# Two of nine blocks take the first MLP layer as seven block products, with state banks returned and remnant units joined

## The chip, the cores and the metric

The kernel runs on one core of a Trainium2 chip. A core has five engines that run side by side, each with its own queue of instructions in a fixed order: TensorE (PE in the profile, its weight loads PEld) multiplies matrices into PSUM, VectorE (DVE) and ScalarE (ACT) compute elementwise, GpSimd (POOL) computes elementwise in SBUF and issues some DMAs, SyncE (SP) issues the others. PSUM has eight banks of 128 x 512 float32. The metric is the device time of one execution in microseconds (us), as the median of several.

## The reference

The inputs are q, k, v of 8 batches, 8 heads, 576 positions and 64 features, and two weight matrices. The first part is a retention: scores with a decay per head, masked to the past, times v. The second is an MLP with the gate h * cos(h) on 4608 tokens.

```python
scores = scale * np.matmul(q, k.transpose(0, 1, 3, 2))
Dmat = np.where(rel >= 0, gamma[:, None, None] ** rel[None, :, :], 0.0)
ret = np.matmul(scores * Dmat[None], v)          # x: [4608, 512]
h = x @ w_in                                     # w_in: [512, 2048]
g = h * np.cos(h)
out = g @ w_out                                  # w_out: [2048, 512]
```

## The kernel before

**Blocks and units.** The tokens are split into nine blocks of 512. Blocks 0 to 7 consist of two units each: a unit is 256 positions of one batch, handled in 64-position chunks with a running state (k transposed times v), so that scores are only needed near the diagonal. Block 8 collects the last 64 positions of all batches; its two remnant units are (0,2) and (1,2). For each unit `load` (line 463) brings q, k and v as float32 into staging tiles `stgq`, `stgk`, `stgv`; POOL casts k and weights q and v by the decay into bf16 tiles (`unit`, lines 454 and 496); k and q are transposed on TensorE for the first blocks and by DMA later. `scores` and `outputs` build "sessions" of small matmuls (line 563), in four quadrants of the array at once: scores into two banks, a mask by VectorE into `pt` tiles (line 599), outputs into two banks, ScalarE's copies into the block's input tile `xt`. The states accumulate in two PSUM banks `ST` that are reserved for the whole kernel; ScalarE copies them to SBUF (`snap`).

**The MLP.** `mlp1` computes the first layer of a block for one of 16 slices of 128 hidden features: four matmuls of 512 columns into a bank (256 columns in blocks 0 to 2, two halves apart), ScalarE's sine with a shift of pi/2 into `cb` (line 745), and VectorE's product of bank and `cb` into the gated tile `gt` (line 748). The second layer of block 0 is plain (`plain2`, line 776). Blocks 1 to 8 take the second layer by seven block products instead of eight (`wino2`, line 862, after Strassen and Winograd): sums of blocks of the gated tile (lines 823 and 829, tiles `s`, on VectorE), sums of blocks of w_out made once (`wsums`, tiles `tw`), seven products P1, P2, P6, P5, P7, P3, P4 into three banks A, B and C, of which ScalarE snapshots three into `sn`, and VectorE adds bank and snapshot into the output tile `os` (line 874). `store` (line 761) sends it out by SP.

**The order.** All of this is a graph of tasks. `Graph.run` is a list planner: it gives each task an estimated start from a modelled duration, free engines, free buffers and a due time (`prio`), and the kernel issues every engine's instructions in the order of these starts. `graph` sets the due times: in round j the second layer of block j is due beside the first layer of block j + 1 and the attention of block j + 2, over a period of 28.8 us. `POOLS` holds the number of buffers of each kind. The planner models the fetching of TensorE's instructions (`FETCH`, `left`), and `warm` fills planned gaps early in the kernel with matmuls on a tile of ones (line 401). The weights w_in and w_out come in four parts each through POOL's DMA queue (`load_w`, lines 717 and 721), each behind a gate: a load that must have landed first.

## Time and profile before

| | |
|---|---|
| median of 3 runs | 301.96 us (301.09 to 302.47) |
| the profiled execution | 301.62 us, its span 299.9 us |
| matmuls of the first layer, 512 columns | 384, 95.4 us busy |
| the same, 256 columns | 384, 49.0 us busy |
| gate products on VectorE, 512 columns | 96, 688 ns each |
| sines on ScalarE, 512 columns | 96, 689 ns each |
| output DMAs | 16 of 512 KB, 4 of 128 KB, 2 of 256 KB |
| granted TensorE clock | 1.000 |

A busy matmul is longer than its slot, since matmuls overlap: the distance between starts is what counts. In the rows of groups, "out<-in" names the tiles written and read, "xN" the number of instructions, and "mean ns" the time that one is shown with. A chain row gives start, length, engine, tile and line.

### The profile page before, as it was taken

The page shows a single profiled execution, that of the slowest core. Times are in us where ns is not written, and L with a number is a line of the kernel's source. Part 1 is how long each engine was busy: PE and PEld are TensorE (multiplying, and loading weights), DVE is VectorE, ACT ScalarE, POOL GpSimd, SP SyncE. Part 2 cuts the span into 40 slices and gives each one's busy share as a digit, 9 for nine tenths or more (in the row PEclk, how much of TensorE's full clock was granted, in tenths as well). Part 3 has the DMA queues.
Part 4 walks back from the last instruction along what each step waited for, and adds up shares of the span by engine and source line. Part 5 has one row for each costly group of instructions (what it writes and reads, how often), then busy time and mean ns, then how long its engine had stood idle before and what let it go on. Part 6 is the DMA issues. An engine that isn't in the chain of part 4 may idle for free.

```text
span 299.9 us, 9086 instructions
## 1 busy us (share of the span) xinstructions
PE 285.2 (95%) x3809; PEld 202.7 (68%) x3815; DVE 213.0 (71%) x379; ACT 169.7 (57%) x315; POOL 101.4 (34%) x125
## 2 busy tenths in 40 slices
PE   6789888999999999999999999999999999999994
PEld 6667665666788876766676667666766666666683
DVE  2776495659985889697868686959777666667721
ACT  5369876556667565645655565466565555545420
POOL 3821960665825614825363515172100000000000
PEclk9999999999999999999999999999999999999999
DMA  7999789999999799997999986892103000300115
GB/s 199 252 203 274 202 129 236 280 200 299 207 251 297 151 194 281 214 227 210 229 280 232 244 188 94 194 236 53 24 2 140 2 2 2 140 2 0 70 73 140
DMA packets 101640, 49.87 MB, mean 166 GB/s; under 512 B 43488, under 2 KB 97248, under 8 KB 101600
## 3 DMA queue, kind: packets, MB, share of 16 engines
q1 hardware_dynamic: 97376, 45.10, 63.6%
q0 software_dynamic: 4224, 4.19, 8.8%
q8 instruction: 30, 0.49, 0.7%
q14 instruction: 10, 0.08, 0.1%
HBM read 36.70 MB, written 9.44 MB: 154 GB/s over the span
## 4 chain that ended last, share of the span: by engine, by line
PE 78%; DMA 14%; POOL 5%; issue 1%; SPq 0%; ACT 0%; DVE 0%; DVEq 0%
PE bk L737 35%; PE bk L862 33%; DMA stgq<-in_q_dram 8%; PE bk L563 6%; DMA wout<-in_moe_w_out_dram 3%; DMA win<-in_moe_w_in_dram 3%; PE bk L776 2%; POOL qnat L496 2%; POOL natv L496 2%; PE st L563 1%; POOL natk L454 1%; SPq L463 0%; POOL win L717 0%; POOL wout L721 0%; DVE qnat L496 0%
## 5 line engine op out<-in xcount | busy, mean ns | idle before, releaser
L745 ACT ACTIVATE cb<-bk,cpi 128x256 bf16<-128x256 f32 (+1 forms) x192 | 108.3, 583 | 82.0 <-PE bk L737 79.9
L737 PE MATMUL bk<-xt,win 128*128 128x256 bf16 (+1 forms) x768 | 144.2, 326 | 1.0 <-DMA win<-in_moe_w_in_dram 0.7
L748 DVE TENSOR_TENSOR gt<-bk,cb 128x256 bf16<-128x256 f32 (+1 forms) x192 | 103.8, 555 | 54.9 <-ACT cb L745 47.8
L737 PEld LDWEIGHTS bk<-xt,win 128*128 128x128 bf16 x768 | 72.3, 98 | 39.7 <-DVE pt L599 1.4
L496 POOL TENSOR_TENSOR natv<-stgv,wv 128x512 bf16<-128x512 f32 x36 | 37.7, 1070 | 37.0 <-PE bk L563 20.6
L599 DVE TENSOR_TENSOR pt<-bk,tr 128x512 bf16<-128x512 f32 x68 | 42.7, 682 | 5.5 <-PE bk L563 5.4
L496 POOL TENSOR_TENSOR qnat<-stgq,wq 128x512 bf16<-128x512 f32 x32 | 35.0, 1112 | 15.9 <-DMA stgq<-in_q_dram 15.3
L454 POOL CAST natk<-stgk 128x512 bf16<-128x512 f32 x34 | 21.3, 653 | 55.8 <-DMA stgk<-in_k_dram 44.8
L862 PE MATMUL bk<-wout,gt 128*128 128x256 bf16 x256 | 32.7, 273 | 0.0
L862 PE MATMUL bk<-tw,s 128*128 128x256 bf16 x256 | 32.7, 273 | 0.0
L862 PE MATMUL bk<-wout,s 128*128 128x256 bf16 x256 | 32.4, 273 | 0.0
L862 PEld LDWEIGHTS bk<-tw,s 128*128 128x128 bf16 x256 | 24.9, 98 | 8.1
L862 PEld LDWEIGHTS bk<-wout,gt 128*128 128x128 bf16 x256 | 24.7, 98 | 6.4
L862 PEld LDWEIGHTS bk<-wout,s 128*128 128x128 bf16 x256 | 24.7, 98 | 6.1
L453 ACT ACTIVATE xt<-bk 128x512 bf16<-128x512 f32 x36 | 23.5, 728 | 0.5 <-PE bk L563 0.5
L874 DVE TENSOR_TENSOR os<-bk,sn 128x512 f32<-128x512 f32 x24 | 16.4, 683 | 10.4 <-PE bk L862 10.4
L453 ACT ACTIVATE sn<-bk 128x512 f32<-128x512 f32 x24 | 14.3, 597 | 13.8 <-PE bk L862 13.8
L862 PE MATMUL bk<-tw,gt 128*128 128x256 bf16 x128 | 16.4, 273 | 0.0
L776 PE MATMUL bk<-wout,gt 128*128 128x512 bf16 x58 | 15.3, 380 | 0.6 <-issue 0.3
L862 PEld LDWEIGHTS bk<-tw,gt 128*128 128x128 bf16 x128 | 12.5, 98 | 4.0
L829 DVE TENSOR_TENSOR s<-gt 128x1024 bf16<-128x1024 bf16 x16 | 12.8, 800 | 0.2
L563 PE MATMUL bk<-qt,kt 64*64 64x128 bf16 (+1 forms) x576 | 12.1, 217 | 0.4 <-ACT xt L453 0.4
(58 smaller groups left out, 187.7 us busy)
## 6 DMA issues: line engine op xcount, KB each, us to landing
stgk<-in_k_dram SPq DMA_DIRECT2D x16, 512.0 KB, 7.0
stgq<-in_q_dram SPq DMA_DIRECT2D x16, 512.0 KB, 6.9
stgv<-in_v_dram SPq DMA_DIRECT2D x16, 512.0 KB, 6.9
out_dram<-os SPq DMA_DIRECT2D x16, 512.0 KB, 3.3
win<-in_moe_w_in_dram POOLq DMA_DIRECT2D x4, 512.0 KB, 9.0
wout<-in_moe_w_out_dram POOLq DMA_DIRECT2D x4, 512.0 KB, 10.0
stgk<-in_k_dram SPq DMA_DIRECT2D x8, 128.0 KB, 3.4
stgq<-in_q_dram SPq DMA_DIRECT2D x8, 128.0 KB, 3.5
```

The costliest lines, as they stand in the source:

```text
L453: return self.one(eng, dur, lambda e: e.activation(dst(), src(), AF.Copy), r=r, w=w, **kw)
L454: return self.one(eng, dur, lambda e: e.tensor_copy(dst(), src()), r=r, w=w, port=True, **kw)
L496: self.one(eng, 610 if eng == "dve" else 1000, lambda e, out=out, inp=inp, tab=tab, col=col, hs=hs: e.tensor_tensor(out(), inp(), ap(tab, ...
L563: return lambda e: e.matmul(out(), lhs(), rhs(), start=start, stop=True, skip_group_check=True)
L599: self.one("dve", 610, lambda e, r=r, b=b, pt=pt: e.tensor_tensor(ap(self.at(pt), 1024, 0, 128, 512 * r, [64 * ny * ny, 8 // ny // ny], [1 ...
L737: inst = e.matmul(ap(self.at(bk), 512, 0, 128, 0, [1, n]), ap(self.WIN, 4 * DFF, 0, 128, c * DFF + 128 * f, [1, 128]), ap(self.at(xt), 204 ...
L745: self.one("act", 70 + n, lambda e: e.activation(ap(self.at(cb), TB, 0, 128, 0, [1, n]), ap(self.at(bk), 512, 0, 128, 0, [1, n]), AF.Sin, ...
L748: self.one("dve", 75 + n / 0.96, lambda e: e.tensor_tensor(ap(self.at(gt), NF * TB, 0, 128, f * TB + 256 * h0, [1, n]), ap(self.at(bk), 51 ...
L776: inst = e.matmul(self.at(bk).ap(), ap(self.at(gt), NF * TB, 0, 128, f * TB + 256 * half + 128 * tt, [1, 128]), ap(self.WOUT, NF * DM, 0, ...
L829: self.one("dve", 610, lambda e, i=i, q=q, x=x, y=y, op=op: e.tensor_tensor(sv(i, q), x(), y(), op), r=r, w=[(S_[i, q],)], port=True, name ...
L862: inst = e.matmul(ap(self.at(bank), 512, 0, 128, 256 * tt, [1, 256]), l(f, tt), rr(f), start=(first and f == 0 and tt == 0), stop=True, sk ...
L874: self.one("dve", 610, lambda e: e.tensor_tensor(view(h, c), ap(self.at(bank), 512, 0, 128, 0, [256, 2], [1, 256]), ap(self.at(sn[name]), ...
```

## The change

**Seven products in the first layer.** From `SEVEN = 7` on, a block's first layer is computed by `seven1` in four groups; a group covers two slices of each half of the hidden features. x and w_in are seen as 2 x 2 blocks (halves of the tokens or of the hidden features, halves of the model features). `wsums1` makes the sums of w_in once (three into new tiles `tx`, one in place over the second half of the hidden features), `xsums` those of the block's input (three into `xs`, one in place in `xt`), all on VectorE. Each of the seven products is four matmuls of 256 columns. ScalarE snapshots three banks; VectorE adds bank and snapshot into a new float32 tile `h` in SBUF; ScalarE takes the sine of it, and VectorE the product. The fourth quarter is gated out of its bank, as before. All products of the gate are on VectorE, as before.

**The second layer.** The third sum of the gated tile is now written in place over the tile; for block 7 the sums go to POOL. In the last block bank A is two banks, and its last product, copies and stores go by halves of tokens.

**Sessions and banks.** The remnant units share one session for their scores and one for their outputs. The state banks are buffers of the pool of eight, free again after their last use.

**Planner and pools.** Instruction fetch is modelled otherwise, warming matmuls have 512 columns instead of 128, w_out is gated by q of unit (1,1) instead of v, and unit (2,0) by the third part of w_out instead of the second. A write of an `h` tile waits for VectorE's own earlier readers of it.

```diff
-            deps += [d for d in readers if d.eng != eng or d.sem or sem]
+            deps += [d for d in readers if d.eng != eng or d.sem or sem or k[0] == "h"]
...
-    AHEAD, FETCH = 2000, 3000
+    AHEAD, FETCH = 2000, 6500
...
+    @staticmethod
+    def fill(gap, seen):
+        return int(0.6 * (gap - 150) / 220 if seen else (gap - 300) / 430)
...
-                if e == "pe" and t.count > left[0]:
-                    s = max(s, left[1] - t.dur * left[0] / t.count)
+                if e == "pe" and t.count:
+                    k = (seen + t.count - 443) // 256
+                    if k >= 0 and 443 + 256 * k > seen and k in asked:
+                        s = max(s, asked[k] + self.FETCH - t.dur * (443 + 256 * k - seen) / t.count)
...
-                dma_free = max(dma_free, s + (1700 if e == "pool" else 1150)) + t.dma
+                dma_free = max(dma_free, s + (2400 if e == "pool" and s > dma_free - 700 else 1700 if e == "pool" else 1150)) + t.dma
...
-    POOLS = dict(bk=6, stgk=3, stgv=3, stgq=3, natk=3, natv=3, qnat=2, kt=3, qt=3, pt=4, sba=3, sbb=3, sbr=8, xt=2,
-                 gt=2, s=9, cb=3, os=3, sn=3)
+    POOLS = dict(bk=8, stgk=2, stgv=2, stgq=2, natk=3, natv=3, qnat=2, kt=3, qt=3, pt=2, sba=3, sbb=3, sbr=8, xt=2,
+                 gt=2, s=6, cb=4, os=2, sn=5, xs=3, h=4)
...
-        self.ST = [nc.alloc_psum_tensor(f"st{i}", [128, 512], F32) for i in range(2)]
...
-                    self.warm(int((gap - 300) / 110 if not warm else 0.6 * (gap - 150) / 57))
+                    self.warm(max(1, self.G.fill(gap, warm)))
...
-                inst = e.matmul(ap(self.at(self.wb), 512, 0, 128, 0, [1, 128]), self.ONE.ap(), self.ONE.ap(),
+                inst = e.matmul(self.at(self.wb).ap(), self.ONE.ap(), ap(self.ONE, 128, 0, 128, 0, [0, 4], [1, 128]),
...
+        if join is not None:
+            join.append((u, phases))
+            if len(join) < 2:
+                return
+            self.emit_lanes("ses/%d.%d" % u, prio, [x for _, y in join for x in y], alloc=[self.tiles[v]["pt", 0] for v, _ in join])
...
+            self.emit_lanes("ses:%d.%d" % u, prio, [(x[0], x[2], x[3], []) for x in join]
+                            + [(x[1], x[2], x[3], [i]) for i, x in enumerate(join)], alloc=[xt])
...
+    def wsums1(self):
...
+        for c in range(2):
+            for dst, x, y, r, w in (
+                    (lambda c=c: t(1, c), lambda c=c: b(0, 1, c), lambda c=c: b(0, 0, c), slabs(0) + slabs(1), [("x1", c)]),
+                    (lambda c=c: t(2, c), lambda c=c: b(1, 1, c), lambda c=c: t(1, c), slabs(1) + [("x1", c)], [("x2", c)]),
+                    (lambda c=c: t(4, c), lambda c=c: b(1, 0, c), lambda c=c: t(2, c), slabs(0) + [("x2", c)], [("x4", c)]),
+                    (lambda c=c: b(0, 1, c), lambda c=c: b(1, 1, c), lambda c=c: b(0, 1, c), [], slabs(1))):
+                self.one("dve", 610, lambda e, dst=dst, x=x, y=y: e.tensor_tensor(dst(), x(), y(), ALU.subtract),
+                         r=r, w=w, port=True)
+
+    def xsums(self, j):
...
+                (1, lambda: a(0, 1), lambda: a(1, 1), self.xkeys(j, (1,)), ALU.add),
+                (2, lambda: sv(1), lambda: a(0, 0), self.xkeys(j, (0,)) + [(X[1],)], ALU.subtract),
+                (4, lambda: a(1, 0), lambda: sv(2), self.xkeys(j, (0,)) + [(X[2],)], ALU.subtract)):
...
+    def seven1(self, j, g, prio, span):
...
+        A, Bb, C = Buf("bk"), Buf("bk"), Buf("bk")
+        sn = {n: Buf("sn") for n in ("p1", "u2", "p5")}
...
+        def gate(h, n, bank, name):
...
+            if name:
+                src = Buf("h")
+                key = (src,)
+                self.one("dve", 610, lambda e: e.tensor_tensor(
+                    self.at(src).ap(), self.at(bank).ap(), self.at(sn[name]).ap(), ALU.add),
+                    r=[(bank,)] + [(sn[name], x) for x in range(2)], w=[key])
+            self.one("act", 620 if name else 580, lambda e: e.activation(
+                self.at(cb).ap(), self.at(src).ap(), AF.Sin, bias=self.CPI.ap(), scale=1.0), r=[key, ("cpi",)], w=[(cb,)])
+            self.one("dve", 610, lambda e: e.tensor_tensor(dst(), two(src), two(cb), ALU.mult),
+                     r=[key, (cb,)], w=[(gt, 8 * n + 2 * g + f, h) for f in range(2)])
+
+        for n, p in enumerate((1, 2, 6, 5, 7, 3, 4)):
...
+            self.one("pe", 4 * 109, mm, r=keys, w=[(bank,)], alloc=[gt], prio=prio + span * n / 7, name=f"M{p}_{j}", count=8.4)
+            if p == 1:
+                snap("p1", A)
+            elif p == 2:
+                gate(0, 0, Bb, "p1")
+            elif p == 6:
+                snap("u2", A)
+            elif p == 5:
+                snap("p5", C)
+            elif p == 7:
+                gate(1, 1, A, "p5")
+            elif p == 3:
+                gate(0, 1, C, "u2")
+            else:
+                gate(1, 0, A, None)
...
     def wino2(self, j, base, span):
...
+        eng, dur = ("pool", 2000) if self.SEVEN <= j < NTB - 1 else ("dve", 610)
+        S_ = {(i, q): Buf("s") for i in (1, 2, 4) for q in range(2)}
...
+            self.one(eng, dur, lambda e, q=q: e.tensor_tensor(a(0, 1, q), a(0, 0, q), a(0, 1, q), ALU.subtract),
+                     r=ak(0, 0, q), w=ak(0, 1, q), port=True, name=f"S3_{j}")
...
+        last = j == NTB - 1
+        A, Bb, C = [Buf("bk") for _ in range(1 + last)], [Buf("bk")], [Buf("bk")]
...
+            halves = last and p == 4
...
-                if j == NTB - 1:
+                if last:
                     self.store(j, 1, os[1], (256, 512))
-                    self.store(j, 1, os[1], (0, 256))
+                    for i in range(2):
+                        self.store(j, 1, os[1], (0, 256), (i,))
...
+        self.stb = [Buf("bk"), Buf("bk")]
...
+            if us[0][1] == 2:
+                self.unit(us[1])
+                one, two = [], []
+                for u in us:
+                    self.scores(u, prio, [], 0, one)
+                for u in us:
+                    self.outputs(u, prio + 10000, [], two)
+                return
...
-        gate = [(st["v", (1, 1)], 0)]
+        gate = [(st["q", (1, 1)], 0)]
...
-        self.unit((2, 0), gate=[("wout", 1, 0)])
+        self.unit((2, 0), gate=[("wout", 2, 0)])
...
+            if j + 1 == self.SEVEN:
+                self.wsums1()
+            if j + 1 >= self.SEVEN and not last:
+                self.xsums(j + 1)
+                for g in range(4):
+                    self.seven1(j + 1, g, base + PER * g / 4, PER / 4)
+            elif not last:
```

## The prediction

> **What bounds the kernel now.** I read the page first (busy shares and slices), then the busy time by stage, then the chain that ended last, then VectorE's own rows. The first fence is from the page, the second the stages: each row has start:end, length, and busy time with count of PE, PEld, DVE, ACT, POOL, then clock, DMA share and GB/s.
>
> ```profile
> span 299.9 us, 9086 instructions
> PE 285.2 (95%) x3809; PEld 202.7 (68%) x3815; DVE 213.0 (71%) x379; ACT 169.7 (57%) x315; POOL 101.4 (34%) x125
> ```
>
> ```profile
> 0.00:17.20 17.20, 12.39 (x264) 10.78 (x264) 8.03 (x28) 8.81 (x15) 10.63 (x25) 1.00 1.00 222
> 17.20:61.00 43.80, 38.49 (x577) 28.18 (x577) 29.83 (x66) 31.37 (x71) 19.24 (x24) 1.00 1.03 218
> 61.00:229.10 168.10, 167.84 (x2325) 117.52 (x2327) 132.73 (x223) 98.47 (x182) 71.48 (x77) 1.00 0.87 195
> 229.10:258.20 29.10, 28.93 (x371) 18.97 (x370) 20.39 (x32) 15.33 (x24) 0.00 (x0) 1.00 0.10 38
> 258.20:282.60 24.40, 24.40 (x164) 15.74 (x162) 17.18 (x26) 12.10 (x18) 0.00 (x0) 1.00 0.08 28
> 282.60:295.70 13.10, 13.10 (x121) 11.52 (x118) 4.84 (x7) 3.08 (x5) 0.00 (x0) 1.00 0.28 90
> 295.70:299.90 4.20, 0.03 (x1) 0.00 (x0) 0.00 (x0) 0.60 (x1) 0.00 (x0) 1.00 0.71 187
> ```
>
> The reader is to see three things. From 61 us to 295.7 TensorE (PE) waits 0.43 us in all, so there the time is the sum of its matmuls. Before 61 us it idles 4.8 and 5.3 us. After its last matmul 4.2 us of copying and storing follow. Block 7's first layer runs in the row 229.1 to 258.2, beside block 6's second layer and the two remnant units; block 8's in 258.2 to 282.6, beside block 7's second layer. VectorE (DVE) is busy 70% of both; POOL does nothing.
>
> The chain of waits is TensorE from 60.85 us to its last matmul (start, length, count):
>
> ```profile
> 61.82 1.31 PE bk L737 x12
> ...
> 262.67 0.86 PE bk L737 x4
> 263.53 0.87 PE bk L862 x8
> ...
> 282.62 13.11 PE bk L862 x120
> ```
>
> Four 512-column matmuls of the first layer take 0.86 us (0.216 each), twelve of 256 columns 1.31, and 120 of 256 columns in the second layer, each with its own weights, 13.11: 0.109 each. Half the columns cost half, so products of blocks lose nothing by their size.
>
> **VectorE's prices.** Timeline of VectorE, then durations by tile (minimum/median/maximum, ns):
>
> ```profile
> 214.15 0.69 DVE L823 TENSOR_TENSOR s<-gt 128x1024 bf16<-128x1024 bf16 x1
> 214.88 0.69 DVE L823 TENSOR_TENSOR s<-s,gt 128x1024 bf16<-128x1024 bf16 x1
> 216.69 2.48 DVE L599 TENSOR_TENSOR pt<-bk,tr 128x512 bf16<-128x512 f32 x4
> ```
>
> ```profile
> L823 DVE TENSOR_TENSOR s<-s,gt x16: 681/691/1421, 73.7 to 284.9; 128x1024 bf16<-128x1024 bf16 x16
> L829 DVE TENSOR_TENSOR s<-gt,s x16: 679/684/1294, 83.1 to 285.6; 128x1024 bf16<-128x1024 bf16 x16
> L874 DVE TENSOR_TENSOR os<-bk,sn x24: 674/681/693, 86.3 to 294.0; 128x512 f32<-128x512 f32 x24
> L496 POOL TENSOR_TENSOR natv<-stgv,wv x36: 1032/1042/1492, 8.8 to 209.3; 128x512 bf16<-128x512 f32 x36
> ```
>
> An instruction is shown with 0.69 us, but four in a queue end after 2.48, so the pitch is 0.60; one that reads its predecessor starts 0.73 after it. Sums with both inputs in SBUF run to 1.42 us and POOL's products to 1.49, where the two engines meet; L874, with one input in a PSUM bank, never exceeds 0.693.
>
> **The change, part by part.** The sum stands against the profiled execution: 301.62 us, 299.9 of it span and 1.7 around it. The median of the three runs is 301.96, 0.34 above, which I add at the end. Times at which a transfer landed are from the trace's records of the DMAs.
>
> *First layer of blocks 7 and 8.* Removed per block: 16 x 4 matmuls x 0.216 = 13.8 us. Added: 4 groups x 7 products x 4 matmuls x 0.109 = 12.2. All of it lies on the path: 2 x 1.6 = 3.2 us less.
>
> *Remnant units joined.* In the timeline their four sessions push the next matmul back by 0.38 and 0.92 us (231.8, 236.6) and again 0.38 and 0.91 (246.3, 251.2): 2.6 us. Joined, the half sessions hide each other's 0.3 us between the main and the cross part, and two seams of 0.11 (a slot of 0.97 instead of 0.86) go. Ends 0 and -0.8; I take -0.5. Four banks are now wanted at once for them; eight are there, with the two state banks back.
>
> *ScalarE.* 24 more snapshots at 0.597 (row sn<-bk, 597 ns) make 14.3 us beside 27.4 busy of 53.5: room, costed at nothing. If that cover went, each would hold the next product of its bank.
>
> *VectorE.* Added in the two stages: 24 additions of a bank and its snapshot at 0.60 = 14.4; eight block sums of the input at 0.42 (nearest row: the copy of 128x512 bf16, 420 ns; between 0.3 and 0.69) = 3.4; two sums of w_in in place, 1.4. Removed: block 7's eight sums, which go to POOL, 8 x 0.69 = 5.5. So 20.4 + 17.2 = 37.6 us becomes 51.3, or some 48.5 when everything queues at the pitch, beside a TensorE need of 53.3 - 3.7 = 49.6. VectorE is then as full as TensorE. Queued behind each addition are the sine of ScalarE (which reads h), the snapshots in ScalarE's order behind that sine, and TensorE's next product into the same bank. The new order of VectorE on itself for h waits for an instruction already ahead of it in the queue and costs nothing.
>
> *POOL beside it.* Eight sums of 1024 columns have no row; by the 1.04 us of 512 columns they take 2.05 each, 16.4 in all, between 0.69 (VectorE's own) and 2.4. Three of four gate products now have both inputs in SBUF (h and cb), as the rows that went to 1.42 had. One that finds POOL at work waits for the rest of its 2.05, 1.0 on average. Ends for TensorE: 0, as with the blocked sums of before (1.29 at 130.3, 1.35 at 208.6), which left no gap on it, and 5.3 (worked out as a rival below). I take +1.2, near the end of those rows, because the second layer's products, 0.87 each, stand between those of the first.
>
> The Trainium skill (SBUF — State Buffer, section "Who interferes with whom") has a rule that speaks against the change: a VectorE instruction with two SBUF inputs and a GpSimd instruction that reads SBUF exclude each other for a whole instruction, and one with a single SBUF input is free of it. The trace agrees: 1.42 and 1.49 us where both are at work, 0.693 at most for L874. By that rule alone 24 products would be exposed and the sum would be the slower rival's; by the uncovered rows it would be 1.2 us lower than mine.
>
> *Sums of w_in.* Six more go wherever VectorE is free once w_in has landed, from 26.6 us on: 6 x 0.69 = 4.1 in a stage where VectorE is busy 29.8 of 43.8. Ends 0 and +1; +0.2.
>
> *The start.* w_out is asked for when q of unit (1,1) has landed (34.85) instead of v (36.38): its four requests (3.0 us on POOL) can go ahead of POOL's two q products (2.06, from 35.16). Either w_out lands up to 2.0 us sooner, or that unit's scores come 3.0 later; SP's loads of unit (2,0) now wait for the third w_out part instead of the second (47.05, 2.5 us before the third), which cancels the gain. The planner's other view of instruction fetch and longer, fewer warming matmuls (103 of 128 columns now) reorder everything before 61 us. What it could win is bounded by the idle 5.3 us there, of which "issue" has 1.8. Ends -2.5 and +1.5; I take -0.6, a third of the issue time.
>
> *Smaller pools.* Output tiles three to two: the store of 135.77 has landed at 139.67, the next sum into that tile is at 147.3; at the end 284.08 against 287.03. Costed at nothing for these leads. Staging three to two, score tiles four to two: units are some 14 us apart; nothing, at most +2 should a load come late, since 0.26 us idle in 61 to 229 shows no other reserve.
>
> *The tail.* The last product is finished by halves of tokens, copied and stored so. The copy shrinks from 0.60 to about 0.38 (128x256 row, sba<-st, 383). But SP issues six requests from 292.99 to 297.69, some 0.64 each when they queue, and there will be eight. Request seven and eight then start about E+1.5 to E+2.2 after TensorE's end E and land 2.3 later, as against E+3.87 now. Ends -0.5 and +0.6; I take +0.2.
>
> Sum: 301.62 - 3.2 - 0.5 + 1.2 + 0.2 - 0.6 + 0.2 = 298.9, plus 0.3 to the median: **299.2 us**.
>
> **The rivals.** *VectorE and POOL hold each other (slower).* While POOL's eight sums run, each lets one gate product through: 2.05 + 0.60 us for a product and an addition that otherwise take 1.20, so 8 x 1.45 = 11.6 us on VectorE, 48.5 + 11.6 = 60.1 against 49.6. TensorE can fill 5.2 us of that with block 8's products that need no late sum (six slots of 0.87), so about 5.3 is lost: 301.6 - 3.7 + 0.2 + 0.2 + 5.3 = 303.6, 303.9 with the median (the start costed at nothing). For it: VectorE's 48.5 of 49.6 us, and an order on TensorE that is fixed beforehand, so that one late product holds all behind it. Against: POOL's first four sums can start when half of block 7 is gated, some 13 us before its second layer begins, and so meet fewer products. It is slower than the median by 0.5% from a stall of 4.9 us on. Chance 0.22.
>
> *The stall eats the gain (within 0.5%).* A smaller stall, 1.9 to 4.9 us: 300.5 to 303.5, say 301.8. Bank A of each group is written, read, written four times; a turn takes 0.2 + 0.6 + 0.2 us, of which a product of 0.44 covers half, and the second layer's 0.87 must cover the rest. Chance 0.18.
>
> *The start gains too (faster still).* If 2.0 to 2.5 us of the idle before 61 us go and no engine stalls: 301.6 - 3.2 - 0.8 - 2.2 + 0.3 = 295.7. For it: 10 us idle before 61. Against: loads and POOL set the chain there. Chance 0.15.
>
> *TensorE doesn't get shorter.* If the seven products ran at more than 0.123 each (13.8/112), nothing would be saved. The 1.31 us row excludes that but for a few in a hundred, held in the second rival.
>
> **How the numbers follow.** The forecast has 0.45, with its own range 297.5 to 300.4. About 0.5% (1.5 us) is what a measurement of this kernel tells from no change: 300.45 and 303.47. Faster: 0.45 + 0.15 = 0.60; same 0.18; slower 0.22. The range that leaves out one in ten on each side is 295.5 to 304.0.
>
> **What would show it.** Right: about 224 matmuls of 256 columns on the new line at 0.109 pitch, TensorE idle under 2 us between 229 us and its end, which comes at 292 to 293; POOL at 16 us there. Wrong: products on VectorE above 1 us whose start falls into a POOL sum, PE waiting for DVE or ACT in stretches of 0.5 us and more; a start in which TensorE idles more than 10 us up to 61 us; loads that release TensorE after 61 us; last store over 4 us after the last matmul.

## The result and the profile after

The changed kernel takes **310.99 us** (median of 6, 308.44 to 311.8) against 301.84 for the kernel before (median of 6, 301.09 to 304.0): ratio 1.0285, 95% interval 1.0247 to 1.0322. It is slower; the forecast was 299.2 us with a range up to 304.0. The profiled execution of the changed kernel took 308.44 us, the least of its six, with a span of 306.6 us against 299.9.

The first lines of the profile's page of the changed kernel:

```profile
span 306.6 us, 9125 instructions
PE 284.8 (93%) x3834; PEld 207.3 (68%) x3834; DVE 236.3 (77%) x412; ACT 179.7 (59%) x342; POOL 123.2 (40%) x133
```

TensorE is as busy as before (285.2 us then), VectorE by 23 us and POOL by 22 us more. The stages of the changed kernel, with the columns of the earlier table (start:end, length, busy time with count of PE, PEld, DVE, ACT, POOL, then clock, DMA share, GB/s):

```profile
0.00:17.20 17.20, 13.08 (x193) 6.94 (x194) 8.80 (x29) 8.82 (x15) 10.65 (x25) 1.00 1.00 224
17.20:61.00 43.80, 39.22 (x570) 27.42 (x568) 31.31 (x67) 30.68 (x70) 21.41 (x25) 1.00 1.08 221
61.00:232.20 171.20, 168.55 (x2331) 117.87 (x2330) 134.17 (x228) 98.62 (x183) 72.08 (x76) 1.00 0.86 190
232.20:290.20 58.00, 52.59 (x644) 45.19 (x643) 55.52 (x80) 37.88 (x67) 19.03 (x8) 1.00 0.10 38
290.20:301.60 11.40, 11.39 (x104) 9.83 (x102) 6.53 (x11) 3.29 (x8) 0.00 (x0) 1.00 0.22 69
301.60:306.60 5.00, 0.00 (x0) 0.00 (x0) 0.00 (x0) 0.38 (x1) 0.00 (x0) 1.00 0.62 158
```

The third row ends where block 7's first layer begins: at 232.2 us, 3.1 us later than before, with 2.65 us of idle TensorE where there was 0.26. The fourth row is the new first layer: TensorE is idle for 5.41 of its 58.0 us, VectorE's instructions cover all but 2.5 us (time spent waiting for POOL included, see below), and POOL works 19 us. The last row, after the last matmul, has grown from 4.2 to 5.0 us. What TensorE waited for in blocks 7 and 8 (view of waits of PE from 228 to 292 us; total, times, longest):

```profile
PE bk L881 <- DVE h L867: 2.7, 3, 1.7
PE bk L1015 <- DVE gt L872: 1.7, 1, 1.7
PE bk L881 <- DVE xs L814: 0.8, 1, 0.8
PE bk L881 <- ACT sn L463: 0.2, 1, 0.2
```

L881 are the seven products of the first layer, L1015 those of the second. All but 0.2 us of the 5.4 is waiting for VectorE. Its timeline there (start, length, tile, and at the end the idle time before):

```profile
251.35 1.34 DVE L872 TENSOR_TENSOR gt<-h,cb 128x512 bf16<-128x512 f32 x1 [0.23 <-ACT cb L870]
...
253.80 1.41 DVE L872 TENSOR_TENSOR gt<-h,cb 128x512 bf16<-128x512 f32 x1
...
256.94 3.35 DVE L872 TENSOR_TENSOR gt<-h,cb 128x512 bf16<-128x512 f32 x2
260.20 1.27 DVE L867 TENSOR_TENSOR h<-bk,sn 128x512 f32<-128x512 f32 x2
...
264.81 2.23 DVE L872 TENSOR_TENSOR gt<-h,cb 128x512 bf16<-128x512 f32 x1
266.96 2.33 DVE L814 TENSOR_TENSOR xs<-xt,xs 128x512 bf16<-128x512 bf16 x1
...
272.36 2.01 DVE L872 TENSOR_TENSOR gt<-h,cb 128x512 bf16<-128x512 f32 x1
```

and POOL's, which has eight instructions there, the sums of block 7's gated tile (four of them shown):

```profile
250.00 2.13 POOL L972 TENSOR_TENSOR s<-gt 128x1024 bf16<-128x1024 bf16 x1 [36.44 <-DVE gt L872]
252.21 2.45 POOL L972 TENSOR_TENSOR s<-s,gt 128x1024 bf16<-128x1024 bf16 x1
...
257.17 2.56 POOL L977 TENSOR_TENSOR s<-gt,s 128x1024 bf16<-128x1024 bf16 x1
264.37 2.13 POOL L972 TENSOR_TENSOR s<-gt 128x1024 bf16<-128x1024 bf16 x1 [4.63 <-DVE gt L872]
```

Every long instruction of VectorE starts inside one of POOL's sums and ends some 0.55 us, nearly its own time, after that sum (the `xs` sum 0.27): 251.35 + 1.34 = 252.69 against POOL's 250.00 + 2.13 = 252.13; 264.81 + 2.23 = 267.04 against 266.50; the pair at 256.94 ends at 260.29 against 259.73. Against the lengths where nothing blocks (0.68 for a product, 1.28 for two, 0.41 for the `xs` sum) the lines above lose 0.66 + 0.73 + 2.07 + 1.55 + 1.92 + 1.33 = 8.3 us. The durations by tile tell which instructions suffer (minimum/median/maximum, ns):

```profile
L872 DVE TENSOR_TENSOR gt<-h,cb x24: 674/684/2604, 243.3 to 290.8; 128x512 bf16<-128x512 f32 x24
L872 DVE TENSOR_TENSOR gt<-bk,cb x8: 674/680/692, 241.5 to 291.4; 128x512 bf16<-128x512 f32 x8
```

The same product of the same size runs up to 2604 ns when both inputs lie in SBUF (`h`, `cb`) and never above 692 when one lies in a PSUM bank (`bk`). The Trainium skill (SBUF — State Buffer, section "Who interferes with whom") has it so: a VectorE instruction with two SBUF inputs and a GpSimd instruction that reads SBUF exclude each other for a whole instruction. The trace agrees, with 2604 against 692 ns.

### The profile page after: what moved, and what is told of

Its sections match the earlier page's. It is cut to its first block, busy times and chain, and to the rows that moved or that the text cites. A ratio compares the mean times of both kernels' runs of the same rounds, so it can differ in the third digit from the quotient of the medians.

```text
span 306.6 us, 9125 instructions
## 1 busy us (share of the span) xinstructions
PE 284.8 (93%) x3834; PEld 207.3 (68%) x3834; DVE 236.3 (77%) x412; ACT 179.7 (59%) x342; POOL 123.2 (40%) x133
## 3 DMA queue, kind: packets, MB, share of 16 engines
q0 software_dynamic: 4224, 4.19, 8.5%
## 5 line engine op out<-in xcount | busy, mean ns | idle before, releaser
L772 ACT ACTIVATE cb<-bk,cpi 128x256 bf16<-128x256 f32 (+1 forms) x160 | 86.5, 565 | 65.2 <-PE bk L764 64.6
L764 PE MATMUL bk<-xt,win 128*128 128x256 bf16 (+1 forms) x640 | 113.3, 316 | 3.2 <-DMA win<-in_moe_w_in_dram 0.8
L775 DVE TENSOR_TENSOR gt<-bk,cb 128x256 bf16<-128x256 f32 (+1 forms) x160 | 81.1, 526 | 42.9 <-ACT cb L772 40.1
L1015 PE MATMUL bk<-wout,gt 128*128 128x256 bf16 x384 | 49.4, 273 | 1.7 <-DVE gt L872 1.7
L1015 PEld LDWEIGHTS bk<-wout,gt 128*128 128x128 bf16 x384 | 36.7, 98 | 9.1 <-DVE gt L872 2.0
L463 ACT ACTIVATE sn<-bk 128x512 f32<-128x512 f32 (+1 forms) x50 | 27.5, 580 | 21.2 <-PE bk L1015 12.2
L1015 PE MATMUL bk<-tw,s 128*128 128x256 bf16 x256 | 32.5, 273 | 0.0
L1015 PEld LDWEIGHTS bk<-tw,s 128*128 128x128 bf16 x256 | 25.0, 98 | 6.3
L872 DVE TENSOR_TENSOR gt<-h,cb 128x512 bf16<-128x512 f32 x24 | 22.4, 951 | 1.1 <-ACT cb L870 1.1
L870 ACT ACTIVATE cb<-h,cpi 128x512 bf16<-128x512 f32 x24 | 16.9, 721 | 6.9 <-DVE h L867 6.8
L1035 DVE TENSOR_TENSOR os<-bk,sn 128x512 f32<-128x512 f32 (+1 forms) x25 | 16.4, 659 | 4.2 <-PE bk L1015 4.2
L1015 PE MATMUL bk<-tw,gt 128*128 128x256 bf16 x128 | 16.4, 273 | 0.0
L1015 PE MATMUL bk<-wout,s 128*128 128x256 bf16 x128 | 16.4, 273 | 0.0
L867 DVE TENSOR_TENSOR h<-bk,sn 128x512 f32<-128x512 f32 x24 | 15.8, 678 | 0.5 <-PE bk L881 0.5
```

The source lines that it names most:

```text
L463: return self.one(eng, dur, lambda e: e.activation(dst(), src(), AF.Copy), r=r, w=w, **kw)
L764: inst = e.matmul(ap(self.at(bk), 512, 0, 128, 0, [1, n]), ap(self.WIN, 4 * DFF, 0, 128, c * DFF + 128 * f, [1, 128]), ap(self.at(xt), 204 ...
L772: self.one("act", 70 + n, lambda e: e.activation(ap(self.at(cb), TB, 0, 128, 0, [1, n]), ap(self.at(bk), 512, 0, 128, 0, [1, n]), AF.Sin, ...
L775: self.one("dve", 75 + n / 0.96, lambda e: e.tensor_tensor(ap(self.at(gt), NF * TB, 0, 128, f * TB + 256 * h0, [1, n]), ap(self.at(bk), 51 ...
L867: self.one("dve", 610, lambda e: e.tensor_tensor(self.at(src).ap(), self.at(bank).ap(), self.at(sn[name]).ap(), ALU.add), r=[(bank,)] + [( ...
L870: self.one("act", 620 if name else 580, lambda e: e.activation(self.at(cb).ap(), self.at(src).ap(), AF.Sin, bias=self.CPI.ap(), scale=1.0) ...
```

## The experiments

Theories at the start: (A) POOL's eight sums hold up VectorE's products, and this costs nearly everything; (B) VectorE is simply too full, whoever makes the sums; (C) the start and the planner cost it; (D) the seven products do not save what was worked out. Each time stands against runs of the kernel before on the same chip, and "excess" is the difference to their median. An excess is known to about 1 us, and to 2 at most where only four executions stand behind it (the runs without seven products, with the old gates, with POOL's sums known, and with short sums at 70 us).

**POOL's sums, an eighth as wide.** The order of every queue is that of the changed kernel; only POOL's instructions are shorter (seven eighths of each sum are left out).

```diff
+        sw = 32 if eng == "pool" else 256
...
-            return ap(self.at(gt), NF * TB, 0, 128, (8 * k + 4 * q) * TB + 256 * h, [TB, 4], [1, 256])
+            return ap(self.at(gt), NF * TB, 0, 128, (8 * k + 4 * q) * TB + 256 * h, [TB, 4], [1, sw])
```

> POOL's eight sums for block 7's second layer cover 128 of 1024 columns (the rest of those sums is left out, so the output is not the reference's); every order and every wait stays as in the changed kernel. Theory A (the wait of VectorE's products for POOL's 2.1 to 2.6 us sums is what costs): the products of h and cb fall to 0.68 us each from up to 2.2, TensorE's idle time after 228 us falls from 6.4 us to under 1.5, and the time falls by 4 to 6 us against the changed kernel, to about 305 median. Rival B (VectorE's load alone, 100% busy from 228 us on, is what costs): TensorE still idles 4 us or more there and the time falls by less than 2 us, to 309 or more.

Measured: 303.84 us (ratio 1.0055, interval 1.0024 to 1.0087), 7.2 us below the changed kernel. VectorE's group and the stage, durations and windows:

```profile
L872 DVE TENSOR_TENSOR gt<-h,cb x24: 678/682/694, 242.5 to 283.5; 128x512 bf16<-128x512 f32 x24
```

```profile
232.20:290.20 58.00, 58.00 (x704) 51.57 (x703) 51.76 (x86) 40.56 (x73) 4.08 (x8) 1.00 0.13 47
```

The longest product falls from 2604 to 694 ns and TensorE has no idle time in the stage. With the same order and the same instructions, the length of POOL's sums is the only thing that differs, so (A) is shown for the 5.4 us of idle time in this stage. What the medians show beyond that is not explained by it; the two profiled executions also differ at 74 us, where the changed kernel's has a gap of 1.88 us and this one none (below). VectorE is still busy 51.8 of 58 us, which speaks against (B).

**The sums back on VectorE.**

```diff
-        eng, dur = ("pool", 2000) if self.SEVEN <= j < NTB - 1 else ("dve", 610)
+        eng, dur = "dve", 610
```

> Block 7's eight sums go back to VectorE, POOL does nothing there. Theory A: VectorE gets 8 x 0.6 to 0.69 = 5 us of work and loses 8.4 us of waits; the time falls by 2 to 4 us against the changed kernel, to 307 to 309. Rival B: VectorE, already full, is 5 us longer, and the time rises by 2 to 5 us, to 313 or more.

Measured: 304.50 us (1.0078, 1.0045 to 1.0111), 6.5 below the changed kernel and more than (A) had expected. The stage's window:

```profile
232.20:290.20 58.00, 58.00 (x703) 51.48 (x702) 55.99 (x95) 41.20 (x72) 0.00 (x0) 1.00 0.14 51
```

VectorE is busier than in the changed kernel (55.99 against 55.52 us, of which 8.3 were waiting), yet TensorE does not wait in this window. (B) falls: load alone was absorbed. The same can be seen over equal work, from the first matmul of block 7's first layer to the last matmul of all; windows of the kernel before, the changed kernel and this run:

```profile
229.13:295.72 66.59, 66.42 (x650) 46.21 (x647) 42.38 (x64) 30.50 (x47) 0.00 (x0) 1.00 0.13 45
```

```profile
232.23:301.60 69.37, 63.95 (x746) 55.00 (x743) 62.02 (x91) 41.16 (x74) 19.03 (x8) 1.00 0.12 43
```

```profile
233.94:297.78 63.84, 63.00 (x746) 55.36 (x743) 58.35 (x99) 41.56 (x74) 0.00 (x0) 1.00 0.13 47
```

With the sums on POOL these 746 matmuls take 5.5 us longer than with the sums on VectorE, where TensorE waits 0.84 us once, near the end, for one of VectorE's own sums. And 63.84 is 2.75 less than before: the seven products do save. But by the medians 304.5 is still 2.4 us above the kernel before, so a second cost exists outside this stage.

**Without the seven products; and with them in block 8 alone.** The rest of the change stays (the eight sums of w_in too). Block 7's sums then stay on VectorE in both.

```diff
-    SEVEN = 7
+    SEVEN = 9
```

The second run has `SEVEN = 8` in its place.

> No block takes the first layer by seven products; all else of the change (pools, state banks, joined remnant units, planner's fetch model, gates of the loads, tail) stays. Theory A (the seven products and POOL's sums are the whole of the loss): 301 to 302, TensorE idle after 61 us under 1 us. Rival C (the rest of the change costs too: TensorE reaches block 7 some 3 us later, and the tail is 0.8 us longer): 304 to 306, with gaps of 1.9 us at 74 us and 0.8 at 204 us as in the changed kernel.

> Only block 8 takes the first layer by seven products; no sums on POOL after the loads. Theory A: the time is that of no seven products less 1.6 us for block 8's first layer. Rival B: VectorE's 12 additions and the sums of x and w_in cost as much or more than that: the time of no seven products or up to 2 us above.

Measured: 307.67 us without (1.0148, 1.0077 to 1.0219), 305.18 with block 8 alone (1.0066, 1.0026 to 1.0105). By the medians, seven products in block 8 save 2.5 us and in both blocks 307.67 - 304.50 = 3.2, the predicted size, though the four runs without them leave it open by about 2 us. With the windows over equal work above, (D) falls: the two blocks and the joined units save 2.75 us there, 3.4 without TensorE's waits. The rest of the change, with the sums of w_in, costs 5.6 us without any seven products, more than either theory had expected: (C) is real beside (A).

**Without the sums of w_in as well.** With `SEVEN = 10` neither the products nor the eight sums are made.

```diff
-    SEVEN = 7
+    SEVEN = 10
```

> As the run without seven products, and without the eight sums of w_in that it still made for nothing; the rest of the change stays. Theory C (pools, planner, gates or tail cost by themselves): 304 to 307.5, with the gap of about 2 us on TensorE at 74 us and, after it, two or three us at half the granted clock; the tail 5.0 us. Rival D (the eight sums of w_in made the loss of that run, by colliding in the start): 301 to 303, and no gap at 74 us.

Measured: 303.91 us (1.0055, 1.0027 to 1.0083). The planner, the gates, the pools, the sessions and the tail cost 1.9 us, and the eight sums of w_in 303.91 to 307.67 = 3.8 more by the medians (3.7 by excess), though VectorE spends only 8 x 0.69 = 5.5 us on them. Each of the two rests on the four executions without seven products. In the profiled execution TensorE still waits at 73.86 us, for 1.03 us and without a loss of clock, where the nearer theory had about 2 us and half the clock. Three runs then each undid one part of this remainder.

**The old planner's costs** (with `SEVEN = 10`): fetching, counts, the narrow warming matmuls and POOL's DMA time as before.

```diff
-    AHEAD, FETCH = 2000, 6500
+    AHEAD, FETCH = 2000, 3000
...
-                dma_free = max(dma_free, s + (2400 if e == "pool" and s > dma_free - 700 else 1700 if e == "pool" else 1150)) + t.dma
+                dma_free = max(dma_free, s + (1700 if e == "pool" else 1150)) + t.dma
...
-                    self.warm(max(1, self.G.fill(gap, warm)))
+                    self.warm(int((gap - 300) / 110 if not warm else 0.6 * (gap - 150) / 57))
```

> The same without seven products or sums of w_in, with the planner's fetch model, the counts and the warming matmuls of before. If these set the order in which VectorE's four sums of block 1 meet POOL's casts at 70 to 75 us, the gap there goes and the time falls by 3 to 4 us against the clean run without seven products, to 301 to 303; if not, it stays within 1 us of that run.

**The old gates** (with `SEVEN = 10`):

```diff
-        gate = [(st["q", (1, 1)], 0)]
+        gate = [(st["v", (1, 1)], 0)]
...
-        self.unit((2, 0), gate=[("wout", 2, 0)])
+        self.unit((2, 0), gate=[("wout", 1, 0)])
```

> The same with w_out behind v of unit (1,1) and unit (2,0) behind the second part of w_out, as before. If the later loads of unit (2,0) are what sets POOL's casts onto VectorE's sums at 70 to 75 us, the gap goes: 301 to 303; if not, within 1 us of the clean run without seven products.

**The old numbers of buffers** (with `SEVEN = 10`; staging 3, score tiles 4, sums 9, outputs 3):

```diff
-    POOLS = dict(bk=8, stgk=2, stgv=2, stgq=2, natk=3, natv=3, qnat=2, kt=3, qt=3, pt=2, sba=3, sbb=3, sbr=8, xt=2,
-                 gt=2, s=6, cb=4, os=2, sn=5, xs=3, h=4)
+    POOLS = dict(bk=8, stgk=3, stgv=3, stgq=3, natk=3, natv=3, qnat=2, kt=3, qt=3, pt=4, sba=3, sbb=3, sbr=8, xt=2,
+                 gt=2, s=9, cb=3, os=3, sn=3, xs=1, h=1)
```

> The same with the buffer counts of before (staging 3, score tiles 4, sums 9, output tiles 3, cb 3, snapshots 3), banks shared as in the change. If fewer staging buffers delay the loads and so POOL's casts, or fewer sum tiles force the four sums into one row, the gap at 74 us goes: 301 to 303; if not, within 1 us of the clean run without seven products.

Measured: 302.71 (1.0004, 0.9973 to 1.0034), 309.11 (1.0201, 1.0146 to 1.0255) and 303.92 us (1.0048, 1.0023 to 1.0074). Against 303.91 the old planner gains 1.2, the old gates lose 5.2, which neither side of the expectation had, and the old numbers of buffers change nothing. So the smaller pools are free, as predicted, and the new gates help in this order. The new planner (fetching, counts, warming and POOL's DMA time together) seems to cost about 1 us instead of gaining; that is the size of the uncertainty, and in the last pair of runs below the same step is worth 0.3 by the medians.

**Where the sums of w_in cost 3.8 us.** The cost does not fall where they run (three at 28 to 37 us, five after 286). The run without seven products has its largest gap at 74 us. PE and VectorE there, timelines (start, length, tile, idle before):

```profile
76.30 0.66 PE L573 MATMUL bk<-qt,kt 64*64 64x128 bf16 x16 [2.26 <-DVE gt L775]
```

```profile
70.45 0.68 DVE L972 TENSOR_TENSOR s<-gt 128x1024 bf16<-128x1024 bf16 x1
71.17 1.42 DVE L972 TENSOR_TENSOR s<-s,gt 128x1024 bf16<-128x1024 bf16 x1
72.51 1.53 DVE L975 TENSOR_TENSOR gt<-gt 128x1024 bf16<-128x1024 bf16 x1
73.97 1.52 DVE L977 TENSOR_TENSOR s<-gt,s 128x1024 bf16<-128x1024 bf16 x1
75.41 0.74 DVE L775 TENSOR_TENSOR gt<-bk,cb 128x256 bf16<-128x256 f32 x2
```

Block 1's four sums stand in a row and meet POOL's q and v products (70.71 to 76.39 us, 1.4 each): they take 5.15 us instead of 4 x 0.69 = 2.8, and the gate products behind them, which give TensorE its banks, are late by the difference. The changed kernel has the same gap with 1.88 us at 74.43. And after the gap the granted clock falls (windows of the same run, columns as in the stage table):

```profile
74.00:76.00 2.00, 0.04 (x1) 0.00 (x0) 2.00 (x4) 0.00 (x0) 2.00 (x2) 1.00 1.52 288
76.00:78.00 2.00, 1.70 (x21) 1.06 (x22) 2.00 (x5) 0.04 (x1) 1.77 (x4) 0.69 0.96 107
78.00:80.00 2.00, 2.00 (x7) 0.90 (x6) 2.00 (x4) 0.77 (x2) 1.78 (x2) 0.50 0.94 204
80.00:82.00 2.00, 2.00 (x20) 1.74 (x19) 1.29 (x4) 1.83 (x5) 0.00 (x0) 0.96 1.01 323
```

TensorE loses 2.26 us idle, then runs two more at 0.69 and two at half the clock; by these slices the clock costs 2 x (0.31 + 0.50 + 0.04) = 1.7 us more, an estimate. To test the place, the same kernel with the first four sums of block 1 an eighth as wide:

```diff
-    SEVEN = 7
+    SEVEN = 9
...
+        for i in range(self.POOLS["s"]):
+            P.add("dve", lambda e, i=i: e.memset(self.mem["s"][i].ap(), 0.0), w=[("s", i)])
...
+        sw = [32 if j == 1 and q == 0 else 256 for q in range(2)]
...
-            return ap(self.at(S_[i, q]), 1024, 0, 128, 0, [256, 4], [1, 256])
+            return ap(self.at(S_[i, q]), 1024, 0, 128, 0, [256, 4], [1, sw[q]])
```

> As the run without seven products that still makes the sums of w_in (307.7), but the first four sums of block 1's second layer cover 128 of 1024 columns (the rest is left out, so the output is not the reference's). If VectorE's meeting with POOL at 70 to 75 us is what stops TensorE there, the gap of 2.3 us goes, the granted clock stays at 1.0 after it, and the time falls by 3 to 4.5 us to 303 to 305. Rival (another wait stands behind it): a gap of over 1 us stays, and the time is above 306.

Measured: 303.89 us (1.0081, 1.0055 to 1.0107), an excess of 2.3 where it was 5.6. Its windows:

```profile
74.00:76.00 2.00, 1.98 (x38) 0.97 (x38) 2.00 (x5) 0.58 (x2) 1.79 (x3) 1.00 1.16 337
...
78.00:80.00 2.00, 2.00 (x21) 1.79 (x19) 1.92 (x6) 1.98 (x5) 2.00 (x3) 1.00 1.47 101
```

No gap, clock 1.00. Four VectorE instructions at 70 us that are 128 columns long instead of 1024 give back 3.3 of the 3.7 us of excess, though the six memsets add 2.8 us to VectorE's first 17. The step from "the sums of w_in are in the order" to "block 1's sums fall on POOL's products" is argued only: without them block 1's sums meet POOL too (the gap of 1.03 us above), the planner's order and the landing times shift together, and no run separates them. The collision also differs between executions: the run with POOL's sums shortened has the changed kernel's order, and its profiled execution shows no wait for `gt` longer than 0.8 us.

**The planner told of the lock.** The planner already keeps instructions marked `port` on VectorE and on POOL apart; the gate products from `h` were not marked.

```diff
-            self.one("dve", 610, lambda e: e.tensor_tensor(dst(), two(src), two(cb), ALU.mult),
+            self.one("dve", 610, lambda e: e.tensor_tensor(dst(), two(src), two(cb), ALU.mult), port=bool(name),
```

> The changed kernel, with one word more for the planner: the gate products whose two inputs lie in SBUF exclude POOL's sums, as the block sums already do. The sums stay on POOL. If the loss in blocks 7 and 8 is that the fixed order did not know of this wait, products above 1 us become rare, TensorE's idle time after 228 us falls from 5.4 us to under 3, and the time falls by 2 to 5 us against the changed kernel, to 306 to 309. Rival (the wait costs VectorE its time whoever knows of it): within 2 us of 311.

Measured: 306.99 us (1.0201, 1.0146 to 1.0256), 4.0 below the changed kernel. The products' mean falls from 951 to 849 ns, and the stage from 232.2 to 290.0 us keeps 2.5 us of idle TensorE. Knowing of the lock gives back part of the loss, taking the sums off POOL more. The planner counts 2.0 us for a sum and the chip takes 2.1 to 2.6; that the planned order fails for this reason is argued only.

**The sums on VectorE, the sums of w_in late.** The six sums of w_in into new tiles wait for the middle of the kernel (they run at 148.9 to 164.5 us), block 7's sums are on VectorE, and the last block ends as before, without halves.

```diff
+        late = [(self.gt[4], 0, 0)]
...
-        eng, dur = ("pool", 2000) if self.SEVEN <= j < NTB - 1 else ("dve", 610)
+        eng, dur = "dve", 610
...
-        last = j == NTB - 1
+        last = False
```

> Block 7's sums on VectorE; the six sums of w_in into new tiles only after block 4's first gate product, so that none is in the start and none in the full stage; the tail as before. Against the run with the sums on VectorE (304.5): the tail gives back 0.8 us, the w_in sums 2 to 3.8 us: 299.5 to 302. Rival: the w_in sums had no part in the gap at 74 us, only the tail comes back: 303.5 to 304.

Measured: **300.41 us** (0.9966, 0.9947 to 0.9985). The stage of blocks 7 and 8 now starts at 230.5 us:

```profile
61.00:230.50 169.50, 167.38 (x2321) 116.54 (x2319) 139.70 (x232) 97.67 (x181) 72.26 (x74) 1.00 0.87 192
230.50:282.90 52.40, 52.40 (x654) 46.55 (x652) 48.97 (x83) 38.98 (x69) 0.00 (x0) 1.00 0.13 47
```

TensorE has no idle time there, and VectorE 3.4 us, with 49 of 52.4 busy. Of the 4.1 us against the sums on VectorE, 0.8 are the tail's (next), and 3.3 are left for the six late sums, near the 3.8 found without seven products. The tail, by the requests of SP's queue at the end, first the changed kernel and then this one (start, time until the last request is issued, count):

```profile
298.92 5.91 SPq L909 DMA_DIRECT2D out_dram<-os  x8
```

```profile
291.46 4.70 SPq L912 DMA_DIRECT2D out_dram<-os  x6
```

TensorE's last matmul ends at 301.60 there and the span at 306.58: 4.98 us, against 298.39 - 294.20 = 4.19 here and 4.17 before. The two added requests lengthen the queue by 1.21 us, 0.6 each. The halves cost 0.8 us.

**The same with the old planner's costs.**

```diff
+        late = [(self.gt[4], 0, 0)]
...
-    AHEAD, FETCH = 2000, 6500
+    AHEAD, FETCH = 2000, 3000
```

> The same with the planner's fetch model, counts and warming matmuls of before. From the run with that planner and no seven products (302.7) less 3.2 for the products and 0.8 for the tail: 298.5 to 300, faster than before by about 1%. Rival: VectorE's load in blocks 7 and 8 takes most of it: 301 to 302.

Measured: **300.08 us** (0.9937, 0.9908 to 0.9967). It is faster than the kernel before by 0.6%, and a ratio of 1 lies outside the interval. Of the 3.2 us that the products save, some 1.6 arrive.

## Why the prediction was wrong

The forecast missed by 11.8 us. Two terms of its sum failed: POOL beside VectorE, taken at +1.2 and measured at 5.4 us of idle TensorE (6.5 by medians), and the sums of w_in, taken at +0.2 and measured at +3.8. The runs divide the miss as follows; each term but the tail is the difference of two medians above, against what the prediction's sum held.

| step | predicted | measured |
|---|---|---|
| first layer of blocks 7 and 8 | -3.2 | -3.2 (without products 307.67, with 304.50) |
| POOL beside VectorE | +1.2 | +6.5 (304.50 to 310.99) |
| sums of w_in | +0.2 | +3.8 (303.91 to 307.67) |
| remnant units, start, pools | -1.1 | +1.1 (303.91 - 302.05 = 1.9, less the tail) |
| tail | +0.2 | +0.8 (4.17 to 4.98) |

The measured terms sum to +9.0, and 301.84 + 9.0 is 310.8. That they add up is no test: the medians form a chain from the changed kernel to the kernel before, so their differences must. The terms of w_in and of the first layer share one median of four executions and are known to about 2 us; the windows over equal work bear out the first layer and POOL's part.

- *First layer.* Right. The slot of four matmuls of 256 columns is 0.43 us in the trace (251.10 to 251.53 on L881), as taken. The saving is worth its size once nothing stalls.
- *ScalarE at nothing.* Right: of the stage's 5.41 us idle only 0.2 end on a snapshot.
- *VectorE's load.* Two sums of w_in were counted in the stage; five ran at 230.7 to 237.6 us, because the in-place sum of the first set of columns, which must wait for block 6's first layer, writes under a key that the sums of the second set read. The total of 48.5 us was near all the same: 55.52 busy less 8.3 of waiting is 47.2. And the load cost nothing in this stage: with all eight sums of block 7 on VectorE as well, TensorE did not wait.
- *POOL beside it.* This step failed most. The duration (2.05 us) was right, 2.13 measured alone, and the lock too. Wrong was the value: +1.2, chosen "near the end of those rows" that showed 1.29 and 1.35 without a gap. One of these in the kernel before:

```profile
208.58 1.35 DVE L829 TENSOR_TENSOR s<-gt 128x1024 bf16<-128x1024 bf16 x1
```

Such a row lost 0.61 or 0.67 us, less than one product of the second layer (0.87) that TensorE has between. Here POOL's instructions were twice as long (2.1 to 2.6 us against 1.04), a row lost up to 2.07, and the fixed order did not always hold enough to cover it: behind the pair at 256.94 the next addition into `h` starts only at 260.20, and TensorE, which has two second-layer products (257.28 and 258.15) to run meanwhile, waits 1.75 us for it. With sums of 0.42 us TensorE lost nothing. VectorE's fullness is not the reason: with the sums on VectorE it had only 2.0 us of 58 free and TensorE did not wait. The slower rival's 5.3 us lost on TensorE equals the 5.4 us of idle in the trace partly by luck: it took 11.6 us lost on VectorE, where 8.3 were, and 5.2 of that as filled by TensorE, where some 2.9 were. Its reason against itself did not hold either: POOL's first four sums began 8 us before block 7's second layer (250.00 against 258.15), not 13, and they met the gate products of block 7's own later groups (its first layer ends at 261 us); the other four, at 264.4 to 273.8, met block 7's last product and block 8's first. By medians the sums on POOL cost 1.1 to 1.8 us more than the idle time seen in the one profiled execution. Four of the six executions have a lower mean clock than that one (next point), so the rest may be clock lost after these waits; no profile shows it.
- *The sums of w_in and the start.* The ends +1 and +1.5 were too near. Only three of the six sums into new tiles ran early (28 to 37 us). The start was bounded by the idle time before 61 us, as though what is reordered there could only be paid there. It was paid at 74 us: block 1's sums against POOL's products, a gap of 1.88 us, and, in the profiles of two related runs, a lower clock after the gap there. How three sums at 28 to 37 us bring this about stays open. Of the changed kernel's six executions the two at clock 1.00 took 308.44 and 309.37 us, the four at 0.990 to 0.994 took 310.75 to 311.8; where their clock fell was not profiled.
- *The new planner.* Taken as a part of -0.6; undone, the time falls by 1.2, at the edge of what the runs can tell. The gates were held to cancel out; undoing them costs 5.2.
- *Remnant units.* The two joined sessions push TensorE's next matmul back by 0.80 and 1.45 us, 2.25 against 2.6: -0.35 where -0.5 was taken.
- *The tail.* The queue of SP was read rightly; 0.8 lies outside the end of +0.6, since the shorter copy gained less than half of what two requests cost.

Of the rivals, that VectorE and POOL hold each other was the right one, with a chance of 0.22, and its 303.9 us was still 7.1 short: it costed the start at nothing, and a second collision of the same two engines, which it did not foresee, came at 74 us.

## What to carry to other kernels

Before work moves to POOL, list VectorE's instructions with both inputs in SBUF that can fall beside it, and charge each POOL instruction's full length to VectorE. VectorE's busy share did not tell here whether that reaches TensorE (55.99 of 58 us without a wait, 55.52 with 5.4): compare the longest single wait with the work that TensorE's fixed order has meanwhile. A row that was blocked for 0.6 us without harm proves nothing for one of 2. A sum that a busy engine can take at 0.6 us was here cheaper than the same sum at 2.1 us on an idle one. Where one fixed order serves the whole kernel, a few added instructions can move a collision elsewhere in it, so the price of an edit is looked for in all stages, the first gaps included.

## What the runs showed of the hardware that was not expected

After a gap of 2.26 us on TensorE the granted clock was 0.69 and then 0.50 for about four microseconds, which by the estimate above cost 1.7 us beside the gap. The run with the old gates shows the same after a gap of 2.37 us that ends at 46.4 us (0.54 and 0.60 in the two slices of 2 us from 46 on) and one of 2.18 that ends at 79.5 (0.58 and 0.57 from 80 on), and the run with the old planner after one of 1.74 that ends at 17.3 (0.59 and 0.56 from 17 on). The length of the gap alone does not decide: the same gap of 1.88 us at 74 us leaves the clock at 1.00 in the profiled executions of the changed kernel, of block 8 alone and of the planner told of the lock, while in that of the sums on VectorE it is 0.50 after it:

```profile
75.82 0.64 PE L573 MATMUL bk<-qt,kt 64*64 64x128 bf16 x16 [1.88 <-DVE gt L775]
```

```profile
76.00:78.00 2.00, 2.00 (x22) 1.10 (x18) 2.00 (x5) 0.47 (x1) 2.00 (x4) 0.50 1.27 139
```

The Trainium skill (TensorE: Matmul & The Clock Gate, "Part 1: The HAM clock gate") ties the half clock to an idle window of about 3.4 us that runs freely; half the clock agrees with the 0.50 here, but the clock fell after gaps shorter than that window.

On POOL a sum of 128x128 takes 0.42 us and one of 128x1024 2.13, so beside VectorE's 0.68 for the same 1024 columns POOL is some three times slower; and while it holds the inputs, VectorE's product waits for nearly the whole of it (2604 ns against 684).
